# Zero products ahead of the opening's transposes, another order for the second batch's last values, and eight output tiles moved from VectorE and GpSimd to ScalarE

## The chip, the cores and the metric

The kernel runs on one core of one Trainium2 chip. A core has TensorE (matrix products, PE in the profile), VectorE (DVE), ScalarE (ACT), GpSimd (POOL), SyncE (SP, used here to issue transfers) and 16 DMA engines. SBUF is the working memory; PSUM holds the results of matrix products. The metric is device time in microseconds (us), lower is better. The kernel before takes 332.1 us, the median of three runs from 331.13 to 332.23.

## The reference, cut to what matters

Sliding-window attention with a linear distance bias on 8 batches of 8 heads, 576 positions of width 64, and then a two-layer network with a swish whose slope is learned per channel.

```python
def _attn_ref(q, k, v):                       # q, k, v: (8, 8, 576, 64)
    B, H, S, D = q.shape
    scores = (1.0 / np.sqrt(D)) * np.matmul(q, k.transpose(0, 1, 3, 2))
    rel = pos[:, None] - pos[None, :]
    slopes = 2.0 ** (-8.0 * (np.arange(H) + 1) / H)
    bias = slopes[:, None, None] * (-np.abs(rel))[None]
    mask = (rel >= 0) & (rel < 128)
    scores = np.where(mask, scores + bias[None], -1e9)
    attn = softmax(scores)                    # over the last axis
    return np.matmul(attn, v)

x = attn_out.transpose(0, 2, 1, 3).reshape(4608, 512)
h = x @ w_in                                  # (512, 2048)
g = h * (1.0 / (1.0 + np.exp(-beta * h)))
out = g @ w_out                               # (2048, 512)
```

All inputs and the output are float32 in device memory; the kernel computes its products in bf16 with float32 sums.

## The kernel before

The work is one long program. The opening makes constants and does the attention of batch 0. A middle stage does batch 1's attention woven into the first product of token group 0. From then on the nine groups of 512 tokens go through the network (`Hm`/`HS`: first product, tanh form of the swish; `OS`: second product) while the attention of later batches is woven in. TensorE, SyncE and GpSimd run their instructions in the order in which the program gives them; ScalarE's and VectorE's order in the later stages is chosen by a scheduler.

A zero product writes PSUM tile `SS`, in which half of the attention scores also land:

```python
    def idle(n):
        for _ in range(n):
            nc.tensor.matmul(
                SS[:, 0, :], lhsT=zeros[:, 0:P], rhs=zeros[:], start=True, stop=True,
                skip_group_check=True)
```

Keys and queries of one pair of heads arrive in float32, are cast by GpSimd (keys first), transposed by TensorE into `tps` and copied out, keys by VectorE and queries by ScalarE:

```python
    def cast_pair(b, p):
        ...
        for i, what in ((1, "k"), (0, "q")):
            r = nc.gpsimd.tensor_copy(out=..., in_=fs.pop((what, b, "p", p))[:])

    def TP(b, p):
        src = staged.pop((b, "p", p))
        for i in (1, 0):
            tps = psum_t.tile([P, FULL], BF16, name="tps", tag="t")
            ...
            for c in range(4):
                nc.tensor.transpose(out=to[:, c], in_=src[:, i, c], identity=ident[:])
            if i:
                nc.vector.tensor_copy(out=QK[b % 2][:, 1, p, 0:FULL]..., in_=tps...)
            else:
                nc.scalar.copy(out=QK[b % 2][:, 0, p, 0:FULL], in_=tps[:])
```

The scores of a pair are made in two visits, "A" into `SS` and "B" into `SX`; ScalarE's exponential empties them:

```python
    def SP_(b, vis, p):
        sps = SX if vis == "B" else SS
        ...                                   # bias product(s), then the score products
        nc.scalar.activation(out=pt[:, :, 0:w], in_=sps[:, :, 0:w], func=ACTF.Exp, scale=qscale)
```

`PVP(b, vis, p)` multiplies weights by values, and VectorE's `norm` (a reciprocal and a product) empties the result; `XP(b, p)` turns the pair's attention output round; `TT`, `SCT`, `PV(b, 4, g)` and `X(b, 4)` do the same for the last 64 positions of a batch. In `factor`, VectorE multiplies weights by the bias and mask factors, both operands in SBUF. The opening's order, cut:

```python
            cast_pair(0, 0)
            TP(0, 0)
            ...
            SP_(0, "A", 0)
            cast_pair(0, 1)
            TP(0, 1)
            ...
            SP_(0, "B", 0)
            SP_(0, "A", 1)
            cast_v(0, 0)
            cast_pair(0, 2)
            w1.append(load_w1(0))
            TP(0, 2)
            M(0)
            SP_(0, "B", 1)
            cast_v(0, 1)
            idle(2)
            SP_(0, "A", 2)
            PVP(0, "A", 0)
            M(1)
            cast_pair(0, 3)
            SP_(0, "B", 2)
            TP(0, 3)
            ...
```

The middle stage. `VB(p)` is `PVP(1, "B", p)`, `VA(p)` is `PVP(1, "A", p)`, `B_(p)` is `SP_(1, "B", p)`, `XO(p)` is `XP(1, p)`, `h[j]` a first product of group 0. `open_o` gives `SX`'s two banks to a pool of two tiles, `pvo` and later `ops`; from there on `VA`, `VB` and `PV(0, 4, ...)` take their result tiles from it in turn:

```python
        steps = [h[2], R(0), h[3], A(0), h[4], R(1), B_(0), h[5], A(1), h[6], R(2), B_(1), VA(0),
                 h[7], A(2), R(3), h[8], VA(1), B_(2), VB(0), h[9], A(3), VB(1), VA(2), h[10],
                 B_(3), open_o, lambda: TT(0), h[11], VA(3), XO(0), lambda: SCT(0), h[12], VB(2),
                 XO(1), h[13], VB(3), lambda: PV(0, 4, 0), h[14], lambda: PV(0, 4, 1), XO(2),
                 half(0), lambda: X(0, 4), XO(3), half(2)]
```

The outputs. A finished tile is halved out of PSUM and stored:

```python
            if last or n == 3:
                osb = osb_pool.tile([P, DM], F32, name="osb", tag="osb")
                o = osb[:, 0 : cols.stop - cols.start]
                if g < 2 or at:
                    nc.vector.tensor_scalar_mul(o, ops_[:, cols], 0.5)
                else:
                    nc.scalar.mul(o, ops_[:, cols], 0.5)
                ...
    def store():
        row0, cols, o = waiting.pop(0)
        g = row0 // TOKG
        eng = nc.gpsimd if g < 2 else nc.sync if row0 >= B * S - 2 * P else nc.scalar
        eng.dma_start(out=out[row0 : row0 + P, cols], in_=o)
```

Of the kernel before, what the change touches and what calls it, by code (L numbers as in the profile page):

```python
# [15 lines left out]
P = 128  # L16
# [3 lines left out]
def kernel(  # L20
# [10 lines left out]
    nc = tc.nc  # L31
    B, H, S, D = q.shape
# [10 lines left out]
    TOKG = 512  # L43
# [59 lines left out]
# [5 lines that stand above are left out]
# [137 lines left out]

    pts, xns = {}, {}

    def TP(b, p):
        src = staged.pop((b, "p", p))
        for i in (1, 0):  # L250
            tps = psum_t.tile([P, FULL], BF16, name="tps", tag="t")
            to = tps[:].rearrange("d (c r) -> d c r", c=4)
            if i == 0:
                to = tps[:].rearrange("d (k c r) -> d c k r", k=4, c=4)
# [3 lines that stand above are left out]
                nc.vector.tensor_copy(  # L258
                    out=QK[b % 2][:, 1, p, 0:FULL].rearrange("d (r c) -> d r c", c=4),
                    in_=tps[:].rearrange("d (c r) -> d r c", c=4))  # L260
            else:
                nc.scalar.copy(out=QK[b % 2][:, 0, p, 0:FULL], in_=tps[:])

    def TT(b):

        src = staged.pop((b, 4))
        tps = psum_t.tile([P, 2, NP, 64], BF16, name="tpt", tag="t")
        for i in range(2):
            for p in range(NP):
                nc.tensor.transpose(  # L270
                    out=tps[:, i, p, :],
                    in_=src[0:64, i, 2 * p : 2 * p + 2, :].rearrange("r h d -> r (h d)"),
                    identity=ident[0:64, 0:64],
                )
        nc.scalar.copy(out=QK[b % 2][:, :, :, FULL:S], in_=tps[:])
# [82 lines left out]
    def SCT(b):  # L358
        qk = QK[b % 2]
        for p in range(NP):  # L360
            for kb, at in ((4, 0), (3, 256)):
                for e in range(2):
                    nc.tensor.matmul(
                        SS[:, e, at + 64 * p : at + 64 * p + 64],
                        lhsT=qk[64 * e : 64 * e + 64, 1, p, P * kb : P * kb + P],
                        rhs=qk[64 * e : 64 * e + 64, 0, p, FULL:S],
                        start=True, stop=True, skip_group_check=True,
                    )
        nc.scalar.activation(
            out=PC[:, 0:1024].rearrange("p (e w) -> p e w", e=2), in_=SS[:], func=ACTF.Exp,  # L370
            scale=qscale)
        nc.vector.tensor_tensor(
            out=PC[:, 0:1024], in0=PC[:, 0:1024], in1=fallt[:].rearrange("k e w -> k (e w)"),
            op=ALU.mult)
# [48 lines left out]
    def PV(b, qb, g):  # L423
        assert ("v", b, qb) in moved
        nq = ROWS[qb]
        vs = VS[b % 2]
        if g == 0:
            xns[b, qb] = xn_pool.tile([P, H, D], BF16, name="xn", tag="xn")
        xn = xns[b, qb]
        if b:  # L430
            pv = psum_t.tile([P, 4, 66], F32, name="pv", tag="t")
        else:
            pv = late["o"].tile([P, 4, 66], F32, name="pvo", tag="ops")
        for hl in range(4):
            h = 4 * g + hl
            if qb:
                nc.tensor.matmul(  # L437
                    pv[:, hl, 0 : D + 1], lhsT=weights(b, qb - 1, h, 1),
                    rhs=vs[:, qb - 1, h, 0 : D + 1], start=True, stop=False,
                )  # L440
            nc.tensor.matmul(  # L441
                pv[:, hl, 0 : D + 1], lhsT=weights(b, qb, h, 0),
                rhs=vs[:, qb, h, 0 : D + 1], start=qb == 0, stop=True,
            )
        norm(xn[0:nq, 4 * g : 4 * g + 4, :], pv, nq)
# [59 lines left out]
    def OS(g, i, n):  # L505
        gT = gts[g]
        if n == 0:
            late[g, i] = late["o"].tile([P, DM], F32, name="ops", tag="ops")
        ops_ = late[g, i][:]
        last = (g, i) == (NTG - 1, 3)  # L510
        for at in ((0, 256) if last else (0,)):
            cols = slice(at, at + 256) if last else slice(0, DM)
            for j in range(NFF) if last else range(4 * n, 4 * n + 4):
                nc.tensor.matmul(  # L514
                    ops_[:, cols], lhsT=gT[:, j, i * P : i * P + P], rhs=W2[:, j, cols],
                    start=(j == 0), stop=(j == NFF - 1),
                )
            if last or n == 3:
                osb = osb_pool.tile([P, DM], F32, name="osb", tag="osb")
                o = osb[:, 0 : cols.stop - cols.start]  # L520
                if g < 2 or at:
                    nc.vector.tensor_scalar_mul(o, ops_[:, cols], 0.5)  # L522
                else:
                    nc.scalar.mul(o, ops_[:, cols], 0.5)  # L524
                row0 = g * TOKG + i * P
                waiting.append((row0, cols, o))

    def store():
        row0, cols, o = waiting.pop(0)
        g = row0 // TOKG  # L530
        eng = nc.gpsimd if g < 2 else nc.sync if row0 >= B * S - 2 * P else nc.scalar
        eng.dma_start(out=out[row0 : row0 + P, cols], in_=o)


# [63 lines left out]
    with tc.manual_schedule(engines={ENG.PE, ENG.SP, ENG.Pool}):  # L598
        with tc.manual_schedule(engines={ENG.Activation, ENG.DVE}):
            for w in ("p0", "p1", "v0", "p2", "v1", "p3", "v2", "v3"):  # L600
                n = int(w[1])
                if w[0] == "p":
                    get_pair(0, n)
                else:
                    get("v", 0, n)
            constants()
            more_constants()
            w1, w2 = [], []
            ones()
            betas()  # L610
            M = lambda p: factor(pts[0, "B", p], None, p)
            cast_pair(0, 0)
            TP(0, 0)
            for h in range(2):
                falls_rows(h)
            SP_(0, "A", 0)
            cast_pair(0, 1)
            TP(0, 1)
            for h in range(2, 5):
                falls_rows(h)  # L620
            SP_(0, "B", 0)
            SP_(0, "A", 1)
            cast_v(0, 0)
            cast_pair(0, 2)
            w1.append(load_w1(0))
            TP(0, 2)
            M(0)
            SP_(0, "B", 1)
            cast_v(0, 1)
# [7 lines that stand above are left out]
            PVP(0, "A", 1)  # L637
            cast_v(0, 2)
            cast_v(0, 3)
            w1.append(load_w1(1))  # L640
            padding()
            PVP(0, "A", 2)
            SP_(0, "A", 3)
            SP_(0, "B", 3)
            PVP(0, "B", 0)
            PVP(0, "A", 3)
            idle(1)
            XP(0, 0)
            PVP(0, "B", 1)
            PVP(0, "B", 2)  # L650
            idle(2)
            PVP(0, "B", 3)
            XP(0, 1)
            XP(0, 2)
            for h in range(5, 8):
                falls_rows(h)
            Hm(0, 0, range(3))
            XP(0, 3)
            falls_tail()
            Hm(0, 1, range(3))  # L660
            for j in range(2):
                Hm(0, j, range(3, 4))
# [76 lines left out]
        B_ = lambda p: lambda: SP_(1, "B", p)  # L739
        VA = lambda p: lambda: PVP(1, "A", p)  # L740
        VB = lambda p: lambda: PVP(1, "B", p)
        R = lambda p: lambda: TP(1, p)
        XO = lambda p: lambda: XP(1, p)
        h = HG(0)
        def open_o():
# [4 lines left out]
        half = lambda c: lambda: Hm(0, 15, range(c, c + 2))  # L750
        steps = [h[2], R(0), h[3], A(0), h[4], R(1), B_(0), h[5], A(1), h[6], R(2), B_(1), VA(0),
                 h[7], A(2), R(3), h[8], VA(1), B_(2), VB(0), h[9], A(3), VB(1), VA(2), h[10],
                 B_(3), open_o, lambda: TT(0), h[11], VA(3), XO(0), lambda: SCT(0), h[12], VB(2),
                 XO(1), h[13], VB(3), lambda: PV(0, 4, 0), h[14], lambda: PV(0, 4, 1), XO(2),
                 half(0), lambda: X(0, 4), XO(3), half(2)]
        for f in steps:
            f()
        done = 0
        h, o = HG(1), two(0) + OG(0, 2) + OG(0, 3) + two(1)
# [10 lines left out]
        for g in range(2, NTG):  # L770
            h = HG(g)
# [43 lines left out]
```

## Time and profile before

| | before |
|---|---|
| time, median of 3 | 332.1 us |
| span of the profiled execution | 331.6 us |
| PE busy | 318.8 us, 96% |
| DVE busy | 201.5 us, 61% |
| ACT busy | 186.8 us, 56% |
| POOL busy | 89.9 us, 27% |

The page gives for each engine its busy time, a row of tenths for 40 equal slices of the span, the clock that TensorE was granted (PEclk), the traffic of the DMA engines, and the chain of work that ended last. Busy time of PE says only that products were in flight, not that they ran at full clock; so the row of the clock and the table by stretches of time must be read beside it. In the timeline each row has a start, a duration, the engine, the line of the kernel, the operation, what it writes and reads, and in brackets the idle time before it and what ended it.

### The profile page before, as it was taken

Reading aid. Unit: us, or ns where it says so; the run is one execution under the profiler, and the core shown is the slowest. Engines: PE = TensorE matmul, PEld = TensorE weight load, DVE = VectorE, ACT = ScalarE, POOL = GpSimd, SP = SyncE. Lnnn points to the kernel's source line nnn. Section 1 sums busy time; section 2 is a strip of 40 time slices with the busy share of each in tenths; the row PEclk is TensorE's granted clock in tenths of the full one; section 3 lists DMA queues with packets and bytes.
Section 4 is the critical chain, followed back from the end, with each engine's and each line's share of the span. In section 5 each row is a group of like instructions: output and inputs, shape, how many; then the busy total and the mean of one; then the engine's idle time right before and its main releaser. Section 6 shows DMA issues by size and latency. Waiting matters only on the chain.

```text
span 331.6 us, 6047 instructions
## 1 busy us (share of the span) xinstructions
PE 318.8 (96%) x2294; PEld 151.0 (46%) x2294; DVE 201.5 (61%) x424; ACT 186.8 (56%) x265; POOL 89.9 (27%) x150
## 2 busy tenths in 40 slices
PE   6989989999999999999999999999999999999995
PEld 2444544443444454444444444444444445444443
DVE  5777877764868883876288628661876267434400
ACT  6759877624418654667467735664677455345511
POOL 4855711426545343322204222232000000000000
PEclk9699999999999999999999999999999999999999
DMA  8999999999999999994859796997021201210021
GB/s 223 239 257 251 180 196 219 200 201 258 218 225 237 175 232 257 195 199 97 205 97 237 154 218 137 212 184 164 18 63 48 72 16 49 55 65 33 3 95 63
DMA packets 147822, 51.80 MB, mean 156 GB/s; under 512 B 135360, under 2 KB 143824, under 8 KB 147792
## 3 DMA queue, kind: packets, MB, share of 16 engines
q1 hardware_dynamic: 139152, 38.29, 64.6%
q0 software_dynamic: 4864, 6.29, 9.7%
q10 hardware_dynamic: 3776, 6.83, 6.1%
q8 instruction: 18, 0.29, 0.4%
q14 instruction: 12, 0.10, 0.1%
HBM read 36.71 MB, written 9.44 MB: 139 GB/s over the span
## 4 chain that ended last, share of the span: by engine, by line
PE 89%; DVE 4%; ACT 3%; DMA 2%; issue 1%; SPq 0%; POOL 0%; ACTq 0%; DVEq 0%
PE ops L514 36%; PE hps L488 34%; PE SS L404 5%; PE hpo L488 2%; PE pv L441 2%; PE pv L437 2%; DMA fst<-in_q_dram 2%; PE tps L256 1%; DVE gT L496 1%; DVE pt L163 1%; PE SX L304 1%; PE xt L460 1%; ACT sig L495 1%; PE SS L293 1%; PE SS L304 1%
## 5 line engine op out<-in xcount | busy, mean ns | idle before, releaser
L514 PE MATMUL ops<-W,gT 128*128 128x512 bf16 (+1 forms) x592 | 138.5, 374 | 0.5 <-ACT osb L524 0.5
L488 PE MATMUL hps<-XT,W 128*128 128x512 bf16 x532 | 133.3, 379 | 0.8 <-DVE gT L496 0.7
L496 DVE SCALAR_TENSOR_TENSOR gT<-sig,hps 128x512 bf16<-128x512 bf16 x133 | 90.3, 683 | 67.1 <-ACT sig L495 66.0
L495 ACT ACTIVATE sig<-hps,beta_h 128x512 bf16<-128x512 f32 x133 | 91.2, 688 | 60.7 <-PE hps L488 55.9
L514 PEld LDWEIGHTS <-gT 128*128 128x128 bf16 x592 | 54.1, 98 | 58.3 <-issue 3.0
L488 PEld LDWEIGHTS <-W 128*128 128x128 bf16 x576 | 50.5, 97 | 55.7 <-issue 6.1
L411 ACT ACTIVATE pt<-SS 128x1024 bf16<-128x1024 f32 x48 | 48.9, 1019 | 21.8 <-PE SS L404 21.8
L230 POOL CAST vs<-fst 128x512 bf16<-128x512 f32 (+1 forms) x40 | 25.5, 638 | 57.2 <-DMA fst<-in_v_dram 47.4
L524 ACT ACTIVATE osb<-ops 128x512 f32<-128x512 f32 (+1 forms) x28 | 16.5, 589 | 42.9 <-PE ops L514 40.0
L215 POOL CAST bst<-fst 128x512 bf16<-128x512 f32 (+1 forms) x32 | 20.7, 646 | 58.0 <-DMA fst<-in_q_dram 50.8
L163 DVE TENSOR_TENSOR pt<-pt,fall 128x1024 bf16<-128x1024 bf16 x24 | 20.9, 871 | 10.1 <-ACT pt L411 10.0
L328 DVE TENSOR_TENSOR xn<-pv,zs 128x256 bf16<-128x256 f32 (+1 forms) x62 | 26.0, 420 | 1.3
L216 POOL CAST bst<-fst 128x512 bf16<-128x512 f32 (+1 forms) x32 | 20.6, 643 | 17.3 <-DMA fst<-in_k_dram 17.2
L158 DVE TENSOR_TENSOR pt<-pt,falls 128x1024 bf16<-128x1024 bf16 x24 | 17.4, 727 | 11.7 <-ACT pt L411 11.6
L441 PE MATMUL pv<-vs,pt 128*128 128x65 bf16 x240 | 21.8, 194 | 0.7 <-DVE pt L163 0.7
L441 PEld LDWEIGHTS <-pt 128*128 128x128 bf16 x240 | 16.6, 97 | 9.2 <-DVE pt L163 0.8
L404 PE MATMUL SS<-qkT 64*128 64x256 bf16 (+2 forms) x240 | 18.9, 252 | 0.3
L437 PE MATMUL pv<-vs,pt 128*128 128x65 bf16 x192 | 18.1, 193 | 0.0
L437 PEld LDWEIGHTS <-pt 128*128 128x128 bf16 x192 | 15.2, 98 | 5.7
L522 DVE TENSOR_SCALAR osb<-ops 128x512 f32<-128x512 f32 (+1 forms) x9 | 5.9, 656 | 19.6 <-PE ops L514 19.6
L404 PEld LDWEIGHTS <-qkT 64*128 64x128 bf16 x240 | 8.0, 94 | 20.5 <-issue 19.5
L327 DVE RECIPROCAL zs<-pv 128x4 f32<-128x4 f32 (+1 forms) x67 | 11.1, 173 | 2.8 <-PE pv L441 2.3
(84 smaller groups left out, 185.1 us busy)
## 6 DMA issues: line engine op xcount, KB each, us to landing
fst<-in_k_dram SPq DMA_DIRECT2D x32, 256.0 KB, 5.5
fst<-in_q_dram SPq DMA_DIRECT2D x32, 256.0 KB, 5.1
fst<-in_v_dram SPq DMA_DIRECT2D x32, 256.0 KB, 4.7
out_dram<-osb ACTq DMA_DIRECT2D x26, 256.0 KB, 2.5
W<-in_moe_w_in_dram POOLq DMA_DIRECT2D x4, 512.0 KB, 7.8
W<-in_moe_w_out_dram POOLq DMA_DIRECT2D x4, 512.0 KB, 11.3
out_dram<-osb POOLq DMA_DIRECT2D x8, 256.0 KB, 4.4
fst<-in_q_dram SPq DMA_DIRECT2D x8, 128.0 KB, 4.0
```

The costliest lines, as they stand in the source:

```text
L163: nc.vector.tensor_tensor(out=x, in0=x, in1=bass.AP(tensor=t.tensor, offset=t.offset, ap=[list(t.ap[0]), [P, 4], [0, 2], [1, P]]), op=ALU. ...
L215: nc.gpsimd.tensor_copy(out=t[0:rows, 0], in_=fs.pop(("q", b, sb))[0:rows])
L230: return nc.gpsimd.tensor_copy(out=VS[b % 2][0:rows, sb, :, 0:D], in_=fs.pop(("v", b, sb))[0:rows])
L328: nc.vector.tensor_tensor(out=xn, in0=pv[0:nq, :, 0:D], in1=zs[0:nq].broadcast_to([nq, 4, D]), op=ALU.mult)
L404: nc.tensor.matmul(o, lhsT=qk[64 * e : 64 * e + 64, 1, p, P * kb : P * kb + P], rhs=qk[64 * e : 64 * e + 64, 0, p, P * kb : P * kb + nq], ...
L411: nc.scalar.activation(out=pt[:], in_=SS[:], func=ACTF.Exp, scale=qscale)
L437: nc.tensor.matmul(pv[:, hl, 0 : D + 1], lhsT=weights(b, qb - 1, h, 1), rhs=vs[:, qb - 1, h, 0 : D + 1], start=True, stop=False,)
L441: nc.tensor.matmul(pv[:, hl, 0 : D + 1], lhsT=weights(b, qb, h, 0), rhs=vs[:, qb, h, 0 : D + 1], start=qb == 0, stop=True,)
L488: nc.tensor.matmul(hps, lhsT=W1[:, c, bass.ts(j, P)], rhs=XT[:, c, c0 : c0 + TOKG], start=(c == 0), stop=(c == NDM - 1),)
L495: gates[g, j] = nc.scalar.activation(out=sig[:], in_=hps, func=ACTF.Tanh, scale=beta_h[:, j : j + 1])
L496: gates["gT"] = nc.vector.scalar_tensor_tensor(out=gts[g][:, j, :], in0=sig[:], scalar=1.0, in1=hps, op0=ALU.add, op1=ALU.mult)
L514: nc.tensor.matmul(ops_[:, cols], lhsT=gT[:, j, i * P : i * P + P], rhs=W2[:, j, cols], start=(j == 0), stop=(j == NFF - 1),)
```

## The change

It has three parts. First, zero products are put ahead of and inside the transposes of head pairs 1 and 2 in the opening: three before the keys of pair 1 and one between keys and queries, and one and one for pair 2. They are meant to keep TensorE occupied where it waits for data. Second, in the middle stage the last two value products of batch 1 (`VB(2)`, `VB(3)`) and the work on batch 0's last 64 positions come in another order, so that their `norm` on VectorE comes earlier. Third, the eight output tiles of groups 0 and 1 are halved by ScalarE and stored from ScalarE's queue, as those of all later groups are, and not by VectorE and from GpSimd's queue.

```diff
-    def TP(b, p):
+    def TP(b, p, fill=0):
         src = staged.pop((b, "p", p))
         for i in (1, 0):
+            if i == 0:
+                idle(fill)
             tps = psum_t.tile([P, FULL], BF16, name="tps", tag="t")
...
-                if g < 2 or at:
+                if at:
                     nc.vector.tensor_scalar_mul(o, ops_[:, cols], 0.5)
                 else:
                     nc.scalar.mul(o, ops_[:, cols], 0.5)
...
         row0, cols, o = waiting.pop(0)
-        g = row0 // TOKG
-        eng = nc.gpsimd if g < 2 else nc.sync if row0 >= B * S - 2 * P else nc.scalar
+        eng = nc.sync if row0 >= B * S - 2 * P else nc.scalar
...
             cast_pair(0, 1)
-            TP(0, 1)
+            idle(3)
+            TP(0, 1, 1)
...
             w1.append(load_w1(0))
-            TP(0, 2)
+            idle(1)
+            TP(0, 2, 1)
             M(0)
...
-                 B_(3), open_o, lambda: TT(0), h[11], VA(3), XO(0), lambda: SCT(0), h[12], VB(2),
-                 XO(1), h[13], VB(3), lambda: PV(0, 4, 0), h[14], lambda: PV(0, 4, 1), XO(2),
-                 half(0), lambda: X(0, 4), XO(3), half(2)]
+                 B_(3), open_o, lambda: TT(0), VB(2), h[11], VA(3), XO(0), lambda: SCT(0), h[12],
+                 VB(3), XO(1), h[13], lambda: PV(0, 4, 0), lambda: PV(0, 4, 1), XO(2), h[14],
+                 XO(3), half(0), lambda: X(0, 4), half(2)]
```

## The prediction, made before the changed kernel ran

> **What bounds the kernel now.** I first read the busy rows of the page, then the table by stretches of time over the opening with the granted clock, then the timelines where TensorE (PE) waits. The page says that PE is busy for 96% of the span:
>
> ```profile
> PE 318.8 (96%) x2294; PEld 151.0 (46%) x2294; DVE 201.5 (61%) x424; ACT 186.8 (56%) x265; POOL 89.9 (27%) x150
> ```
>
> So only 331.6 - 318.8 = 12.8 us of PE idle time exist, and some 5.5 of them lie at the very start (1.19 us before the first product) and at the end (4.4 us in the last stretch, which the change doesn't touch). What can be won is the remaining 7 us, and time in which PE is busy at a low clock. The table by stretches shows that; its columns are stretch, length, PE, PEld, DVE, ACT and POOL busy, PE clock, DMA share, GB/s:
>
> ```profile
> 4.45:7.86 3.41, 2.08 (x20) 1.13 (x19) 1.43 (x4) 2.11 (x5) 1.45 (x3) 0.98 1.06 288
> 7.86:11.27 3.41, 3.04 (x25) 1.56 (x24) 2.46 (x5) 2.18 (x3) 2.79 (x5) 0.50 1.16 285
> 11.27:14.69 3.42, 3.42 (x24) 1.31 (x23) 2.18 (x3) 2.25 (x4) 3.22 (x5) 0.52 1.15 204
> 14.69:18.10 3.41, 3.06 (x42) 1.58 (x40) 2.98 (x8) 2.56 (x4) 2.97 (x6) 1.00 1.15 296
> ```
>
> The clock is halved at 7.86 us and comes back at 14.69, after two stretches of 3.41 us. Why it fell, and what the zero products will meet, is in the timeline of PE and ACT:
>
> ```profile
> 6.16 0.34 PE L304 MATMUL SS<-qkT 64*128 64x256 bf16 x4 [0.35 <-ACT qkT L262]
> 7.49 0.43 PE L256 MATMUL tps<-ident,bst 128*128 128x128 bf16 x4 [0.98 <-POOL bst L222]
> 8.28 0.40 PE L256 MATMUL tps<-ident,bst 128*128 128x128 bf16 x2 [0.37 <-POOL bst L222]
> ...
> 6.54 0.81 ACT L311 ACTIVATE pt<-SS 128x768 bf16<-128x768 f32 x1 [0.43 <-PE SS L304]
> ...
> 10.66 0.81 ACT L311 ACTIVATE pt<-SS 128x768 bf16<-128x768 f32 x1 [0.16 <-PE SS L304]
> 11.62 0.58 ACT L262 COPY qkT<-tps 128x512 bf16<-128x512 bf16 x1 [0.15 <-PE tps L256]
> ```
>
> The reader is to see two waits of PE for casts (0.98 and 0.37 us), and that the exponential reads `SS` until 7.35 us and again until 11.47 us. In the middle stage and in the stretch of batch 2's first scores the waits are these:
>
> ```profile
> 46.81 0.20 PE L437 MATMUL pvo<-vs,pc 128*128 128x65 bf16 x1 [0.90 <-DVE xnp L328]
> 49.91 0.23 PE L460 MATMUL xt<-ident,xn 64*128 64x64 bf16 x2 [0.77 <-DVE xn L328]
> ...
> 82.92 0.54 POOL L532 DMA_DIRECT2D out_dram<-osb  x1 [1.45 <-DVE osb L522]
> 83.24 3.05 DVE L163 TENSOR_TENSOR pt<-pt,fall 128x1024 bf16<-128x1024 bf16 x1 [0.61 <-ACT pt L411]
> 86.34 0.24 PE L441 MATMUL pv<-vs,pt 128*128 128x65 bf16 x2 [0.67 <-DVE pt L163]
> ```
>
> One factor product took 3.05 us where the median of its line is 0.69, and PE waited 0.67 us for it.
>
> **What the Trainium skill says.** "TensorE: Matmul & The Clock Gate", Part 1 (the clock gate): the array runs at half clock by default and is let up or down according to how busy it was in a free-running window of 3413 ns. The trace agrees: the half-clock time of 6.83 us is two such windows, and the first eight zero products, 3.42 us for eight or 0.43 each, ran at half of what four 128x512 products take later (0.86 for four). No run here shows the threshold. The same page, Part 4 (PE-mode transpose), says that transposes do not count as busy in the same way. That fits 7.86 to 11.27: PE is busy for 3.04 of 3.41 us, a good part of it transposes, and the clock does not rise. "SBUF — State Buffer", section "Who interferes with whom": a VectorE product with both inputs in SBUF contends with GpSimd's reads for a shared pair of ports, and the second to issue is blocked. The trace agrees: four GpSimd casts follow one another from 83.46 to 85.74, and the 3.05 us product ends 0.55 us after the last.
>
> **Part 1, the zero products.** They write `SS`. So the three ahead of pair 1's keys cannot start at 6.50, where PE falls idle, but only when the exponential has read `SS`, at 7.35; the built program indeed has the first of the three wait for ScalarE. Of the 0.98 us wait they fill almost nothing; they start at about 7.40, and two of them, 0.43 us, lie in the window that ends at 7.86. Counting columns of the timeline that are not transposes (bias products in full, 64-row score products half), that window has 1340 columns before, 0.56 us at full clock or 16% of it. It gets about 2430, 30%. The quietest window that held full clock later (14.69 to 18.10) has 54% by the same count. Thus 30% lies between a window that failed and one that held, and I cannot read from this profile which it will be.
>
> If the clock holds: three products at 0.216 end at 8.05, four transposes (0.22) at 8.27, one zero product at 8.49, the queries' transposes then, whose cast ended at 8.23. Their copy starts at 8.9, as before (8.93). Pair 1's second exponential ends near 11.36 (before 11.47). But the zero product ahead of pair 2 waits for exactly that exponential, so PE idles from 9.8 to 11.4; pair 2's queries are transposed at 12.06 and copied at 12.45 (before 11.62, 0.8 later). Then full clock pays: the exponential of A2 starts at 14.05 (before 14.21), B2 at 14.92 (15.44), the copy of pair 3's queries at 15.94 (16.36), B3 at 17.8 (18.24). I take -0.4 us for the opening. Of the 3.3 us that half clock costs PE (6.7 halved), the rest is lost to waits for ScalarE.
>
> If it doesn't hold: the third zero product and the one between keys and queries cost 0.43 each, the queries' transposes end at 9.5 and not at 8.9, A1's exponential ends at 12.36 (+0.9), and pair 2's transposes, behind two more zero products, end at 14.1 and not at 11.6, which is +2.5. The window to 14.69 is then too quiet to lift the clock, and another 3.41 us run at half: in all +2.5 to +4, I take +3.2.
>
> From 22 us on PE is almost never idle, so that either sum goes into the end almost whole. The data for batch 1 allow it: its pair 2 is cast by 30.2 us and needed at 31.9.
>
> **Part 2, the order of the middle.** It aims at the 0.90 and 0.77 us waits. VectorE's norm of `VB(2)` came behind the tail's factor product, which waited for ScalarE until 44.9; with `VB(2)` earlier it comes before. But `VB(2)` now takes the first tile in `SX`'s banks directly after batch 1's last score products, and the exponential that reads them runs from 41.38 to 42.40: PE, ready at 41.51, waits 0.94 us, where before `h[11]` (0.86) filled that time. Then `PV(0, 4, 0)` waits for the factor product, done near 46.6 (0.2 us), and `PV(0, 4, 1)` directly behind it needs the tile of `VB(3)`, whose norm follows a swish product and ends near 47.8: 0.9 us. The stage ends at 50.6 to 50.8 against 50.74. I take -0.1.
>
> **Part 3, the outputs.** Removed: eight VectorE copies of 0.69 (5.5 us) and eight GpSimd issues of 0.54 (4.3 us), with 1.45 us of GpSimd waiting at 82.92. Added: eight ScalarE copies of 0.60 and issues of 0.34, by the rows of later groups, 7.5 us in a stretch where ScalarE is idle for over half (70 to 100 us: 9.9 busy of 30). GpSimd's casts then don't bunch behind a store that waits, and the 3.05 us product should be near 0.9. That gives back the 0.67 us and perhaps 0.2 of small waits. Against it stands one exponential at 82.19 that comes behind a ScalarE copy: +0.13. I take -0.7.
>
> **The rivals.** (1) The clock holds: -0.4 - 0.1 - 0.7 = -1.2, with room for another microsecond if ScalarE's chain closes up better: 330.8. For it speaks that zero products did lift the clock twice (to 4.45, and to 14.69 with two of them inside), and that the fill ahead of pair 2 only makes sense where a gap was seen at full clock. (2) The clock falls as before and the zero products are dead weight: +3.2 - 0.8 = +2.4, 334.5. For it speaks the wait on `SS`. (3) The load moves to ScalarE and exponentials come late, 1 us or so; its idle time of 40.0 us ahead of the later output copies speaks against that. (4) Transfers: 64.6% of the DMA time is SyncE's queue and bounds the arrival of batches 2 and 3; if PE comes early it would wait there. Batch 2's last transposed keys land near 75 us and are needed at 83, so a microsecond or two is free.
>
> **Range and chances.** I give (1) about 65% and (2) about 30%. The middle of the mixture is 331.0 us. The range 328.8 to 334.8 takes in (1) with another 2 us and most of (2). 2% is 6.6 us; all PE idle time outside start and end is 7.3, so faster by over 2% gets 0.02, slower by over 2% 0.02, within 2% 0.96.
>
> **What would show it.** In the table by stretches: the clock from 7.9 to 14.7, 1.00 or 0.50 (the step that decides). In the timeline: the first added zero product at about 7.4 and not at 6.5; the one ahead of pair 2 right after an exponential on `SS`; `VB(2)` waiting near 0.9 us for ScalarE; no factor product over 1.2 us between 75 and 90 us. I am wrong if the zero products start earlier, if the middle gains over 0.5 us, or if PE gains new waits after 60 us.

## The result and the profile after

The changed kernel takes 346.5 us (346.01 to 347.43, 4 runs), the kernel before beside it 332.05 us (331.13 to 332.23, 4 runs): a ratio of 1.0444, 95% interval 1.0413 to 1.0476. The profiled execution spans 345.6 us against 331.6. First the busy row and the clock row of the changed kernel's page:

```profile
PE 320.7 (93%) x2300; PEld 151.4 (44%) x2300; DVE 193.6 (56%) x416; ACT 191.4 (55%) x273; POOL 85.0 (25%) x142
PEclk9999999996699999999999999999999999999999
```

PE is busy for 1.9 us longer than before and idle for 24.9 us, where it was 12.8. The new hole in the clock row is at slices 10 and 11 of 40, about 78 to 95 us. The opening, where the prediction looked for its risk, is at full clock (table by stretches of the changed kernel, columns as in the prediction):

```profile
4.76:8.17 3.41, 2.16 (x20) 1.32 (x21) 1.43 (x4) 1.81 (x4) 1.47 (x3) 1.00 1.10 302
8.17:11.58 3.41, 2.14 (x26) 1.19 (x25) 2.35 (x4) 2.21 (x3) 2.97 (x5) 1.00 1.16 289
11.58:15.00 3.42, 3.42 (x44) 1.75 (x41) 2.83 (x5) 2.47 (x4) 2.58 (x5) 1.00 1.29 216
```

Its PE timeline shows the predicted waits there and in the middle, at nearly the predicted times, and then two long waits that the prediction did not have:

```profile
7.44 0.81 PE L105 MATMUL SS<-zeros 128*128 128x512 bf16 x3 [0.90 <-ACT pt L313]
...
11.21 0.38 PE L105 MATMUL SS<-zeros 128*128 128x512 bf16 x1 [1.27 <-ACT pt L313]
...
42.34 0.40 PE L345 MATMUL pvo<-vs,pt 128*128 128x65 bf16 x8 [0.89 <-ACT pt L313]
...
82.98 1.87 PE L516 MATMUL ops<-W,gT 128*128 128x512 bf16 x4 [5.65 <-ACT osb L526]
...
92.43 0.61 PE L406 MATMUL SS<-qkT 64*128 64x256 bf16 x4 [5.23 <-ACT pt L413]
```

Batch 2's first scores start at 75.97 us, before at 75.92: up to there nothing is lost against that profile. The score product that started at 87.38 before starts at 101.44. So 14.0 us, the whole difference of the spans, are lost between 76 and 101 us, and nothing is given back. 10.9 us are the two waits shown; most of the rest goes with the half clock of this stretch. The table by stretches, first of the kernel before, then of the changed kernel:

```profile
80.00:90.00 10.00, 9.19 (x70) 4.12 (x71) 8.20 (x12) 4.74 (x5) 5.51 (x9) 1.00 1.15 255
```

```profile
70.00:80.00 10.00, 7.33 (x39) 2.99 (x38) 1.52 (x4) 1.28 (x2) 4.43 (x8) 0.98 1.19 196
80.00:90.00 10.00, 3.68 (x12) 1.10 (x12) 0.69 (x1) 2.11 (x3) 3.45 (x6) 0.67 1.16 208
90.00:100.00 10.00, 7.33 (x37) 2.72 (x37) 2.38 (x5) 4.58 (x5) 3.58 (x6) 0.67 1.20 240
```

From 80 to 90 us PE is busy for 3.68 us, VectorE for 0.69 and ScalarE, which they wait for, for only 2.11. An engine that everyone waits for and that is idle itself is standing. What it stands at is in ScalarE's own timeline, with its queue (ACTq) beside it:

```profile
72.62 0.60 ACT L526 ACTIVATE osb<-ops 128x512 f32<-128x512 f32 x1 [1.36 <-PE ops L516]
81.92 0.37 ACTq L533 DMA_DIRECT2D out_dram<-osb  x1
82.33 0.60 ACT L526 ACTIVATE osb<-ops 128x512 f32<-128x512 f32 x1 [9.11 <-DMA fst<-in_q_dram]
83.89 0.36 ACTq L533 DMA_DIRECT2D out_dram<-osb  x1
84.31 1.02 ACT L413 ACTIVATE pt<-SS 128x1024 bf16<-128x1024 f32 x1 [1.38 <-DMA qkT<-bst]
85.23 0.59 ACT L526 ACTIVATE osb<-ops 128x512 f32<-128x512 f32 x1
90.97 0.34 ACTq L533 DMA_DIRECT2D out_dram<-osb  x1
91.35 1.02 ACT L413 ACTIVATE pt<-SS 128x1024 bf16<-128x1024 f32 x1 [5.53 <-DMA fst<-in_q_dram]
```

The first copy is done at 73.22, but its store goes out only at 81.92; the next copy, which needs nothing but a product finished long before (in e3, below, the same copy runs at 73.38), comes behind it. The bracket says what ended the wait: not a product, but the landing of a *load of q*, `fst<-in_q_dram`, which has nothing to do with an output. After the third copy it is the same again. The loads are SyncE's; its timeline in the changed kernel:

```profile
75.41 2.73 SPq L194 DMA_DIRECT2D fst<-in_q_dram  x1
...
79.48 2.06 SPq L384 DMA_TRANSPOSE qkT<-bst  x1
...
86.17 0.63 SPq L194 DMA_DIRECT2D fst<-in_q_dram  x1
```

The built program says why. Each transfer is given a completion counter, and those issued by SyncE and ScalarE share eight of them (DMAHW0 to 7), dealt out in turn. An issue waits until the last transfer that used its counter has landed. The instructions concerned, ScalarE's first three stores and three instructions of SyncE, with the counters they wait for:

```
ACT  67 L533 DMACopy out_dram<-osb 128x512 [waits DMAHW7_49,Activation_49]
ACT  69 L533 DMACopy out_dram<-osb 128x512 [waits DMAHW1_49,Activation_49]
ACT  72 L533 DMACopy out_dram<-osb 128x512 [waits DMAHW5_49,Activation_49]
SP   55 L194 DMACopy fst<-in_q_dram 128x8x64 [waits DMAHW7_49]
SP   57 L384 DmaTransposeAnt qkT_78<-bst 128x8x128 [waits DMAHW1_49,DVE_49,Pool_49]
SP   61 L194 DMACopy fst<-in_q_dram 64x8x64 [waits DMAHW5_49]
```

The counters of the three stores, 7, 1 and 5, were last given to exactly these three transfers of SyncE, issued at 75.41, 79.48 and 86.17 us. And the three waits on ScalarE end with a load of q, a transpose `qkT<-bst` and a load of q, in this order. In program order these transfers stand before the stores; in time SyncE is behind: it is still issuing earlier loads, and its transposes wait for casts. In the kernel before, the eight stores came from GpSimd and used counters of a second set (DMASW0 to 7), whose last users, the loads of weights, had landed long ago.

### The profile page after: what moved, and what is told of

Its sections match the earlier page's. It is cut to its first block, busy times and chain, and to the rows that moved or that the text cites. A ratio compares the mean times of both kernels' runs of the same rounds, so it can differ in the third digit from the quotient of the medians.

```text
span 345.6 us, 6057 instructions
## 1 busy us (share of the span) xinstructions
PE 320.7 (93%) x2300; PEld 151.4 (44%) x2300; DVE 193.6 (56%) x416; ACT 191.4 (55%) x273; POOL 85.0 (25%) x142
## 4 chain that ended last, share of the span: by engine, by line
PE 83%; ACT 4%; DVE 4%; SPq 4%; DMA 3%; issue 1%; POOL 0%; ACTq 0%; DVEq 0%
PE ops L516 33%; PE hps L490 32%; PE SS L406 4%; SPq L194 2%; PE hpo L490 2%; PE pv L443 2%; PE SS L105 2%; PE pv L439 2%; SPq L384 1%; DMA fst<-in_q_dram 1%; DMA fst<-in_k_dram 1%; ACT pt L313 1%; ACT pt L413 1%; PE tps L258 1%; DVE gT L498 1%
## 5 line engine op out<-in xcount | busy, mean ns | idle before, releaser
L516 PE MATMUL ops<-W,gT 128*128 128x512 bf16 (+1 forms) x592 | 141.3, 379 | 6.1 <-ACT osb L526 6.1
L526 ACT ACTIVATE osb<-ops 128x512 f32<-128x512 f32 (+1 forms) x36 | 21.3, 591 | 61.3 <-PE ops L516 52.2
L215 POOL CAST bst<-fst 128x512 bf16<-128x512 f32 (+1 forms) x32 | 20.3, 633 | 66.5 <-DMA fst<-in_q_dram 61.3
L163 DVE TENSOR_TENSOR pt<-pt,fall 128x1024 bf16<-128x1024 bf16 x24 | 17.2, 715 | 31.6 <-ACT pt L413 31.5
L158 DVE TENSOR_TENSOR pt<-pt,falls 128x1024 bf16<-128x1024 bf16 x24 | 18.8, 785 | 12.1 <-ACT pt L413 12.0
L216 POOL CAST bst<-fst 128x512 bf16<-128x512 f32 (+1 forms) x32 | 20.1, 630 | 18.2 <-DMA fst<-in_k_dram 17.9
L222 POOL CAST bst<-fst 128x512 bf16<-128x512 f32 x16 | 10.2, 656 | 4.3 <-DMA fst<-in_k_dram 3.1
```

Of the source, the lines that this page charges most:

```text
L215: nc.gpsimd.tensor_copy(out=t[0:rows, 0], in_=fs.pop(("q", b, sb))[0:rows])
L516: nc.tensor.matmul(ops_[:, cols], lhsT=gT[:, j, i * P : i * P + P], rhs=W2[:, j, cols], start=(j == 0), stop=(j == NFF - 1),)
```

## Experiments

Theory A: the loss is the stores' wait for shared counters on an engine that also has to compute. Rival B: ScalarE is overloaded by eight more copies. Rival C: the stores, taking counters from SyncE, delay SyncE's loads and so batch 2. Beside these, the three parts were to be separated. The ratios are to the kernel before, run beside each experiment: its median was 331.4 us for e1 to e4 and 331.63 us for the later ones.

**e1: parts 1 and 2 only.** Against the changed kernel:

```diff
-                if at:
+                if g < 2 or at:
...
-        eng = nc.sync if row0 >= B * S - 2 * P else nc.scalar
+        g = row0 // TOKG
+        eng = nc.gpsimd if g < 2 else nc.sync if row0 >= B * S - 2 * P else nc.scalar
```

> The changed kernel with part 3 undone (outputs of groups 0 and 1 copied by VectorE and stored from GpSimd's queue again), the zero products and the middle's order kept. Every theory that puts the loss into part 3 expects 331.5 to 332.8 us: the trace after stands at 75.97 us where the one before stands at 75.92 (batch 2's first scores). A theory that the opening or the middle leaves something behind that breaks out later (an earlier or later arrival of batch 2's data) expects 340 or more.

Measured: 333.41 us, ratio 1.0068 (1.0046 to 1.0090). The 14 us are gone, so they belong to part 3. Some 2 us remain, more than was expected; p1 and p2 below find about 1.5 of them by the medians.

**e2: part 3 only.** The kernel before with the opposite edit.

> The kernel before with part 3 alone. Theory A (a store on ScalarE's queue waits until a completion counter is free whose last user is a SyncE transfer that comes late, and ScalarE stands meanwhile): 344 to 347 us, waits of TensorE for ScalarE of 5 us and more between 75 and 95 us, and stores that go out seconds-of-microseconds after their copies (8 to 9 us for the first). Theory that the parts only hurt together: 331 to 334.

Measured: 342.81 us, ratio 1.0346 (1.0318 to 1.0374). That is most of the loss, but less than the 344 to 347 us expected. Its ScalarE timeline, without zero products or another order, stands at the same place, for 6.1 us at the first store (71.90 to 77.96) and not for 8.7:

```profile
71.30 0.60 ACT L524 ACTIVATE osb<-ops 128x512 f32<-128x512 f32 x1 [1.36 <-PE ops L514]
77.96 0.37 ACTq L531 DMA_DIRECT2D out_dram<-osb  x1
78.37 0.60 ACT L524 ACTIVATE osb<-ops 128x512 f32<-128x512 f32 x1 [6.48 <-DMA fst<-in_q_dram]
```

**e3: copies on ScalarE, stores on GpSimd.** The changed kernel with the line of the stores alone put back:

```diff
-        eng = nc.sync if row0 >= B * S - 2 * P else nc.scalar
+        g = row0 // TOKG
+        eng = nc.gpsimd if g < 2 else nc.sync if row0 >= B * S - 2 * P else nc.scalar
```

> The changed kernel, copies on ScalarE, stores of groups 0 and 1 back on GpSimd's queue. Theory A: the loss is gone, 331 to 332.5 us, and no wait of TensorE for a ScalarE copy. Rival B (eight more copies of 0.6 us overload ScalarE, exponentials come late): stays at 340 to 347.

Measured: 332.59 us, ratio 1.0037 (1.0025 to 1.0050). ScalarE does all the copies and the 14 us are gone (the 1.2 us left are about what parts 1 and 2 cost): rival B falls.

**e4: copies on VectorE, stores on ScalarE.** The changed kernel with the line of the copies alone put back (`if g < 2 or at:`).

> The changed kernel, copies back on VectorE, stores still on ScalarE's queue. Theory A: ScalarE stands at its stores again, so exponentials come late: 338 to 347 us, the wait of TensorE for the copy (5.6 us) gone, waits for exponentials of several us left. Rival B: 331 to 333, since ScalarE has no copies any more.

Measured: 347.83 us, ratio 1.0474 (1.0438 to 1.0509), as slow as the whole change, with not one copy of groups 0 and 1 on ScalarE. Its ScalarE timeline:

```profile
71.25 0.69 ACT L497 ACTIVATE sig<-hps,beta_h 128x512 bf16<-128x512 f32 x1 [1.52 <-PE hps L490]
84.81 1.51 ACTq L533 DMA_DIRECT2D out_dram<-osb  x2
86.37 1.02 ACT L413 ACTIVATE pt<-SS 128x1024 bf16<-128x1024 f32 x1 [14.44 <-DMA qkT<-bst]
```

The first two stores go out together at 84.81, the bracket names a transpose, and the exponential that ran at 76.30 in e3 comes at 86.37. e3 and e4 together leave only the issuing of the stores as the cause.

**e5: copies on ScalarE, stores on SyncE.** The counters come from the same eight, but the engine that issues computes nothing.

```diff
-        eng = nc.sync if row0 >= B * S - 2 * P else nc.scalar
+        g = row0 // TOKG
+        eng = nc.sync if g < 2 or row0 >= B * S - 2 * P else nc.scalar
```

> The changed kernel with the copies on ScalarE and the stores of groups 0 and 1 on SyncE's queue, which shares the same completion counters but does no computing. Theory A (what costs is that ScalarE stands at the wait): loss gone, 331.5 to 334 us, perhaps some 0.34 us per store more on SyncE. Rival C (stores through these counters delay SyncE's loads or their data, whoever issues them): 338 or more.

Measured: 332.41 us, ratio 1.0037 (1.0017 to 1.0057), as e3. Rival C falls: stores that take counters from SyncE do not delay its loads by much. The run does not show what a wait for a late load costs on SyncE. In its built program the first three stores take other counters, whose last users (two transposes and a load of v) SyncE has itself issued earlier. With e3 and e4 it leaves this: what costs is that an engine with exponentials to compute issues in order behind a transfer that SyncE hasn't issued yet.

**e10: group 0's stores on GpSimd, group 1's on ScalarE.** This asks whether a store from ScalarE costs by itself.

```diff
-        eng = nc.sync if row0 >= B * S - 2 * P else nc.scalar
+        g = row0 // TOKG
+        eng = nc.gpsimd if g < 1 else nc.sync if row0 >= B * S - 2 * P else nc.scalar
```

> The changed kernel with group 0's four stores back on GpSimd and group 1's four left on ScalarE. In the built program the first two of group 1 wait for the counters of two loads of q that SyncE issues, without disturbance, at about 84 and 88 us, while the copies come at about 91 and 92 us. The theory of the counters says they are nearly free: under 1 us of standing at each, 332.3 to 333.8 us, as with all stores on GpSimd (332.59). A rival in which each store from ScalarE costs by itself, whatever SyncE does, has half of the loss left: about 339 us.

Measured: 333.0 us, ratio 1.0046 (1.0025 to 1.0066). The first two stores of group 1 go out as soon as their copies are done; the two loads that they wait for had been issued by SyncE at 84.08 and 88.27 us. ScalarE's timeline:

```profile
90.60 0.60 ACT L526 ACTIVATE osb<-ops 128x512 f32<-128x512 f32 x1 [1.10 <-PE ops L516]
91.22 0.37 ACTq L534 DMA_DIRECT2D out_dram<-osb  x1
...
92.56 0.59 ACT L526 ACTIVATE osb<-ops 128x512 f32<-128x512 f32 x1
93.18 0.34 ACTq L534 DMA_DIRECT2D out_dram<-osb  x1
```

The same instruction on the same queue is free 10 us later, when the transfers before it have been issued and have landed. The loss is that of group 0's stores alone, as the counters say. No run gave group 0's stores other counters and left all else; e10 comes nearest to that.

**c0: the kernel before once more.** The prediction had taken the fall of the clock in the one profile of before as given.

> The kernel before once more, for its clock in the opening. In the trace of before the clock fell from 7.86 to 14.69 us; in the run of before with part 3 alone, whose opening is the same, it did not fall (full clock from 6.08 on) and the first products of the network began 2.2 us earlier (20.69 against 22.86). Theory: where the free-running window lies decides it, so the clock may or may not fall here; if it falls for two windows the span is near 331.6 us, if not it is near 330.

One profiled execution of 333.38 us, span 331.6 again, where about 330 was expected. The clock rose late, at about 7.1 us (the eight transposes at 4.93 took 1.03 us, in before 0.79), and then did not fall. The table by stretches reads 1.00 there from 4 us on, but it counts the time before the first rise as full clock. PE reaches group 0's first product into `hps` at 20.87 us, before at 22.86. Of this lead of 1.99 us only 0.92 are left at batch 2's first scores (75.00 against 75.92), since the next product of group 0 waits for a copy by VectorE. The fourth factor product, at 0.87 us and not at 3.05, raises the lead to 1.77 (a score product at 85.61 against 87.38). A new wait for a transposing transfer of `XT` takes what is left, so that the same span comes out:

```profile
22.87 0.38 PE L488 MATMUL SX<-XT,W 128*128 128x512 bf16 x1 [1.19 <-DVE XT L355]
...
228.32 1.02 PE L488 MATMUL hps<-XT,W 128*128 128x512 bf16 x4 [1.43 <-DMA XT<-xn]
```

```profile
82.32 0.87 DVE L163 TENSOR_TENSOR pt<-pt,fall 128x1024 bf16<-128x1024 bf16 x1 [0.69 <-ACT pt L411]
```

So both the fall of the clock and the 3.05 us product, on which the prediction built, belong to one execution and are not what the kernel does as a rule. The fall is rare: 6.83 us at half clock take 0.01 off the mean clock of a run (6.83 x 0.5 / 331.6), and of 65 runs of the kernel before beside the later experiments only two have a mean clock of 0.99; they took 334.1 us, where the median is 331.63.

**p1: part 1 only.** The kernel before with the zero products of the change.

> The kernel before with part 1 alone. By the prediction's working at held clock: 0.4 us faster. By what the other runs show (an opening without the added zero products at held clock is at 20.69 us where one with them is at 22.22, of which some 0.4 is lost again by 24 us): 1 to 1.6 us slower than before, 332.4 to 333.0.

Measured: 332.78 us, ratio 1.0050 (1.0031 to 1.0069). The clock held, as in c0, and PE reaches group 0's first product into `hps` at 22.48 us against 20.87 in c0, the middle at 42.31 against 41.53. Against an opening whose clock holds the zero products lose time: 1.6 us at the end of the opening, of which 0.8 is left later. Why is in its PE timeline:

```profile
7.69 0.81 PE L105 MATMUL SS<-zeros 128*128 128x512 bf16 x3 [0.90 <-ACT pt L313]
...
11.46 0.38 PE L105 MATMUL SS<-zeros 128*128 128x512 bf16 x1 [1.27 <-ACT pt L313]
```

**e6: part 1 only, added zeros in a spare tile.**

```diff
+    def fill_other(n):
+        if n:
+            z = psum_h.tile([P, 512], F32, name="zz", tag="hps")
+            for _ in range(n):
+                nc.tensor.matmul(z[:], lhsT=zeros[:, 0:P], rhs=zeros[:], start=True, stop=True)
...
-                idle(fill)
+                fill_other(fill)
...
-            idle(3)
+            fill_other(3)
...
-            idle(1)
+            fill_other(1)
```

> Part 1 alone, with the four added zero products writing a spare PSUM tile that no engine reads, so that they no longer wait for the score tile's exponential to have read it (0.90 and 1.27 us of PE's idle time with part 1 alone, which came to 332.78 us against 331.63). Theory W, the wait is what part 1 costs: about 1 us comes back, 331.3 to 332.2 us. Theory Z, the products' own time and the order they force cost it: 332.5 to 333.2 us, as part 1 alone. In both the clock should stay at 1.00 from 8 to 12 us.

Measured: 331.70 us, ratio 0.9999 (0.9984 to 1.0014): theory W. The PE timeline has the zeros at once and without a wait, and later the transfer again:

```profile
6.64 0.82 PE L113 MATMUL zz<-zeros 128*128 128x512 bf16 x3
...
9.08 0.39 PE L113 MATMUL zz<-zeros 128*128 128x512 bf16 x1
...
227.40 1.02 PE L496 MATMUL hps<-XT,W 128*128 128x512 bf16 x4 [1.33 <-DMA XT<-xn]
```

In this execution batch 2's first scores start at 74.34 us, 0.66 before those of c0 and 1.44 before those of p1; the 1.33 us at 227.40 take it back. Why is open: e8, e9 and p2 start the same product earlier (226.40 to 226.78 us) and without a wait.

**p2: part 2 only.**

> The kernel before with part 2 alone. By the prediction: 0.1 us faster. By the trace after, in which the middle ended 0.25 us later against its own start: 0.2 to 0.5 us slower, 331.6 to 332.

Measured: 331.99 us, ratio 1.0008 (0.9996 to 1.0020). By time it can't be told from nothing. The traces are finer: from the transposes of `TT(0)`, the last work ahead of the new order, to the first output product it is 19.06 us in before, c0 and p1, and 19.30 in p2, e1, e3 and the changed kernel. So the order costs 0.24 us.

**e8 and e9: the copies alone.** Only ScalarE's copies, put into the kernel before; e8 leaves the stores on GpSimd, e9 puts them on SyncE with e5's line. The edit of both:

```diff
-                if g < 2 or at:
+                if at:
```

> The kernel before with only the output copies of groups 0 and 1 moved from VectorE to ScalarE, the stores left on GpSimd. The theory of the completion counters says that the copies alone cost nothing: 331.0 to 332.3 us, ratio 0.998 to 1.003, PE waiting for ScalarE's exponentials under 0.5 us between 70 and 110 us. The rival that ScalarE is overloaded by eight copies of 0.60 us says above 334 us.

> The kernel before with the copies of groups 0 and 1 on ScalarE and their stores on SyncE: the shared counters are the same as with stores on ScalarE, but the engine that stands for them computes nothing. The theory says 330.8 to 332.3 us. If the stores harm by delaying SyncE's loads and transposes behind them, 334 us or more.

Measured: e8 331.30 us, ratio 0.9979 (0.9966 to 0.9992); e9 331.05 us, ratio 0.9980 (0.9965 to 0.9995). Both beat the kernel before by 0.2% (0.7 us by the ratio, 0.3 and 0.6 by the medians) and the changed kernel by some 15 us. That is what the third part was good for, once the stores stay off ScalarE's queue. Where this gain arises was not followed up.

## Why the prediction was wrong

- **The step that failed: part 3, "eight ScalarE copies of 0.60 and issues of 0.34".** The issue was costed by its duration, taken from later groups. Its wait was not asked for, and it is 8.7 us at the first store (73.22 to 81.92) and some 5 at the third. e2 has most of the loss without the other parts (11.4 us by the medians), e4 all of it without the copies, e3 and e5 have the copies without the loss. The copies themselves are about well sized: e8 gives -0.7 us by the ratio (-0.3 by the medians), and -0.7 was predicted. That the size fits is luck. The reason given was the 3.05 us product, and c0 has it at 0.87 with the stores still on GpSimd, while in e9, without any store on GpSimd, one factor product takes 2.19 us. In "SBUF — State Buffer", section "Who interferes with whom", the Trainium skill says that such a product contends with a GpSimd instruction that reads SBUF, and that the order of issue decides which of them is blocked. The trace agrees only in part: the 3.05 us product ends 0.55 us after four casts, but it started at 83.24, ahead of the first of them (83.46). Why it took so long stays open.
- **Rival 3** came nearest ("exponentials come late, 1 us or so") and was dismissed by ScalarE's idle time. Idle time says that an engine has room for more busy time. It says nothing of an instruction that stands in its queue: e4's ScalarE is idle for 14.44 us and is the bottleneck.
- **Rival 4** left the transfers free. Right for the arrival of batch 2, but in e6 and c0 PE does wait for a transfer near 228 us (1.33 and 1.43). Its 64.6% is a share of the span of the 16 engines, not of the DMA time.
- **Part 1, the mechanism** was right: the zeros start at 7.44 (predicted 7.40), the one ahead of pair 2 waits for the exponential (11.21, predicted 11.4), the clock held. Against the profile that it was reckoned from, the size was about right as well: -0.64 at the first product into `hps` (22.22 against 22.86), where -0.4 was taken. But that opening runs 6.8 us at half clock, which most runs do not. Against the runs of before beside it part 1 costs 0.5% (p1), 1.2 us by the medians and 1.7 by the ratio, and e6 shows that the wait on `SS`, which the prediction named, is what costs it.
- **The step from the opening to the end** ("either sum goes into the end almost whole") did not hold. c0 has 1.99 us in hand after the opening and 0.92 at batch 2's first scores; p1's loss against c0 shrinks from 1.6 to 0.8 over the same stretch.
- **Part 2:** `VB(2)` waits 0.89 (predicted 0.94); the sum was -0.1, measured +0.24 in the traces. It left out a wait of 0.29 us for VectorE's copy of the last `XT` columns (before the product at 50.87 in the changed kernel). Nothing hung on it.
- **The range** was too narrow for a reason that isn't one of its terms: all rivals were sized by what PE could gain or lose inside the opening and the middle. "New waits after 60 us" stood among the signs of error and had got almost no chance.

## What to carry to other kernels

Before a transfer is moved to an engine that also computes, ask what the issue must wait for, not how long it takes: look up in the built program which transfers share its completion counter, and whether the queue that issues them runs late. An engine that has to keep pace should issue only transfers whose predecessors have landed; a late store belongs to a queue with nothing behind it. And take a second profile of the kernel before, before an oddity of the first is counted as something to be won.

## What the runs showed that was not expected

- Eight counters are shared by the transfers of SyncE and ScalarE, and one in program order can hold up the other: 8.7 us at a store whose data was ready. The Trainium skill, "DMA: Bandwidth & Descriptors", section "Why a DMA increments its semaphore by 16 and not by 1", shows that with two transfers in flight on one semaphore a wait can pass before the first has fully landed, and asks for one semaphore per slot in flight. The wait that this program has before each issue keeps to that, and here is what it costs. The same page, "Issuing engines are not separate DMA queues", says that issuing from several engines only saves the time of initiating. Here the choice of the engine made 14 us of 332 (e3 and e5 against the changed kernel), because of what the issue waits for.
- The opening's clock is a matter of the execution. Without added zeros it fell for two windows in the first profile of before, for one in p2, and not in c0, e2, e8 or e9. With them it held in the changed kernel, e1, p1, e3, e5, e10 and e6, and fell in e4 for one window. In every trace the clock changes only at whole multiples of 3.41 us after its first rise, and the first rise comes at another moment each time. In the three that fell it came at about 4.2 (e4), 4.3 (before) and 4.6 us (p2). In the eight in which it came at 5.1 us or later the clock held, but it held also in three with an early rise (e9 at 4.0, e6 at 4.4, the changed kernel at 4.5). So where the quiet stretch lies between these moments seems to matter; how busy PE must be was not measured.
- A stall costs twice: with PE idle for 11.7 us of the 30 from 70 to 100, the clock was at half for two times two windows, and the products that did run took longer (1.87 us for four output products, 1.03 at full clock).
